# Attention with random features, a dense block and an eight-expert layer on one core: the first token search is spread anew over the products beside it

## The chip, the cores and the metric

One core of one Trainium2 chip runs the whole program in one launch. The metric is device time in microseconds (us), from the first to the last instruction of an execution and what lies around it. Five engines work at once, each through its own instructions in order: TensorE (PE in rows of the profile; PEld is its loading of weights), VectorE (DVE), ScalarE (ACT), GpSimd (POOL), and SyncE (SP), which here only issues DMAs. An engine waits for another through semaphores.

## The reference, cut to what matters

```python
# 1. attention with random features (4 batches, 8 heads, 576 positions, 64 wide, 128 features)
q_p, k_p = phi(q * scale), phi(k * scale)        # phi: exp of projections on omega, less their maximum
kv = einsum('bhsm,bhsd->bhmd', k_p, v);  z = sum(k_p, axis=2)
x = einsum(q_p, kv) / (einsum(q_p, z) + 1e-6)    # -> 2304 tokens of 512
# 2. dense block, 512 -> 2048 -> 512
h = x @ w_in;  x = (h * clip(h + 3, 0, 6) / 6) @ w_out
# 3. eight experts, each takes cap = 2304 // 8 = 288 tokens, by descending logit
logits = x @ w_gate
for idx in argsort(-logits.flatten()):           # best pair of token and expert first
    tok, e = idx // 8, idx % 8
    if assigned[tok] >= 0 or counts[e] >= cap: continue
    assigned[tok] = e; counts[e] += 1
for e in range(8):
    mask = assigned == e
    out[mask] = maximum(x[mask] @ w1[e], 0) @ w2[e]     # 512 -> 1024 -> 512
```

## The kernel before

Every large product is made three times, on a high and a low part of each operand (`mm3`, L208 to L210): high by high, low by high, high by low. A high part is a rounding copy on ScalarE, a low part a subtraction on VectorE or GpSimd. So each weight tile costs a "split" ahead of its products.

**Dense block.** Tokens go in four blocks of 512 and a short block of 256 (block 4, tiles 16 and 17). `steps` lists 16 jobs per block; `step(i)` makes the first product of job i (`st_A`), and some jobs later the second (`st_B`). The short block keeps its activations (`kept`: gHk, gLk) and makes its second products at the very end, in `rest()`: 16 jobs f, for each two token tiles j, for each three products of 128x512 (L694 and L696 in the two kernels): 96 products, each one `yield`. The weights of job f are split by `st_wo(f)` (L509 the high part oH on ScalarE, L510 the low part oL): on VectorE for f < OD and on GpSimd from there. oH and oL have three buffers, so the high part of job f + 3 waits until the products of job f are done. The finished tiles leave by `st_x` (L570 copy, L572 writes to `xd` in DRAM).

**Logits.** For the first LT = 14 token tiles they are dot products on VectorE (`st_dot`, L581), for the last four products on TensorE (`st_lg`, L611 and L612), which at the end are copied (L615), turned by four small transposes (L618) and added into `lg` (128 partitions x 18 tiles x 8 experts). L714 adds 0.0 to all of `lg`, so that no logit is a negative zero: the search compares the bits of the logits.

**Searches.** `finds()` is one generator for all eight searches. Each finds the expert that fills up next, the value that its 288th token has, and the list of its tokens:
- `begin()`: best logit of each token (L728 maximum), a sortable key, six digits of it, and `cmp`, the first digit compared with all its values (L755).
- `closest()`: six rounds, one per digit. In a round TensorE counts tokens per value with 18 small products (L771), VectorE compares the counts with 288 (`ge`, L773), TensorE sums that up (L776, the threshold product), VectorE takes the largest (dk, L780), makes the next digit's value (v, L783) and the next `cmp` (L755).
- `slots()` (L857, L858: the membership products) and `numbers()` (one-hot rows OH, L889; 18 products, L893) make the list of tokens `idx` (L898).

At each place where TensorE is about to get work of a search the generator yields a name: "cmp0", "cmp5" or "cmp6" ahead of the 18 counting products (by the width of the digit), "ge" ahead of the threshold product, "mem" ahead of membership, "OH" ahead of the 18 products of the list (in searches 0, 1, 6 and 7).

**What sets the order.** On TensorE these parts stand as the program writes them (`manual_schedule`); on the other engines a scheduler sorts by priority. Two tables tell how many products of other work stand behind each name. GAP0 holds for the first search, which is laced into `rest()`: `begin` products ahead of its first step, then after each named step as many as the table says. GAP holds for the searches 1 to 7, which are laced into the experts; there the count is in triples of products (`visit()`; an expert is 64 triples). Between them stands the only part without products of other work: after the first list, `fetch_x(0, ...)` gathers the first expert's rows from `xd` (three gathers, L917, issued by GpSimd), L923 copies the expert's number onto a gathered value so that the remaining weight loads come after the gathers (L925 reads it on SyncE, L928 and L909 load), N1 steps of the second search run, and `prep()` transposes the gathered rows (L943) and splits them (L944, L945). Then `mlp()` runs expert after expert, each with `prep` of the next at triples 56 to 62, and `finish` of the last. Weights We of an expert are split at L959 and L962 (w1), L963 and L966 (w2).

Of the kernel before, what the change touches and what calls it, by code (L numbers as in the profile page):

```python
# [9 lines left out]
ALU = mybir.AluOpType  # L10
# [10 lines left out]
def fused(tc, q, k, v, omega, w_in, w_out, w_gate, w1, w2, out):  # L21
    nc = tc.nc
# [8 lines left out]
    GI, NT = 20, 18  # L31
# [2 lines left out]

    ET = mybir.EngineType
    MN, IC = 16, 32
    OD, WG, ND, NE, XS = 4, 18, 3, 3, 3
    LB, LL, GB = 2, 3, 3

    LT = 14  # L40

    GAP0 = dict(begin=22, cmp5=8, cmp6=9, ge=3, mem=6, OH=0)


    W1C, W2C, Z0 = 4, 4, 2
    FZ, FS, PZ, PS = 6, 2, 56, 2
    HPF, RP, N1, GAP = 400, 30, 8, dict(cmp0=12, cmp5=4, cmp6=5, ge=1, mem=8, OH=9)
    DM = H * D
    DFF = w_in.shape[1]
    N = B * S  # L50
# [3 lines left out]
    with ctx:  # L54
# [9 lines left out]
        def ps(tag):  # L64
            if tag == "big":
                turn[0] += 1
                tag = ("s8", "kv", "kv")[turn[0] % 3]
            tag = TG.get(tag, tag)
            return pp.tile([P, 512], F32, tag=tag, name=tag, bufs=PA[tag])
# [457 lines left out]
        lg = cp.tile([P, NT, 8], F32, name="lg")  # L527
# [72 lines left out]
        def st_lg(i):  # L600

            ib, f = steps[i]
            gH, gL = gs[i]
            if "lg" not in keep:
                keep["lg"] = ps("tp")
            nl = (NT - LT) * P

            o = keep["lg"][:16, 0:nl - 2 * P] if ib < NB else keep["lg"][:16, nl - 2 * P:nl]
            w = wgp[:, f].rearrange("p a e -> p (a e)")
            c = slice((LT - 4 * ib) * P if ib < NB else 0, len(blocks[ib]) * P)  # L610
            nc.tensor.matmul(o, w, gH[:, c], start=f == 0, stop=False, skip_group_check=True)  # L611
            nc.tensor.matmul(o, w, gL[:, c], start=False, stop=f == NF - 1, skip_group_check=True)  # L612
            if ib == NB and f == NF - 1:
                t8 = mp.tile([16, nl], F32, name="lgT", bufs=1)
                nc.vector.tensor_copy(t8, keep["lg"][:16, :nl])  # L615
                pt = ps("tp")
                for j in range(NT - LT):
                    nc.tensor.transpose(pt[:, 16 * j:16 * j + 16], t8[:, j * P:(j + 1) * P], ident[:16, :16])  # L618
                p4 = pt[:, 0:16 * (NT - LT)].rearrange("p (t a e) -> p t a e", t=NT - LT, a=2)
                nc.vector.tensor_copy(lg[:, LT:NT], p4[:, :, 0])  # L620
                nc.vector.tensor_tensor(lg[:, LT:NT], lg[:, LT:NT], p4[:, :, 1], ALU.add)

        def st_B(i):
            ib, f = steps[i]
# [21 lines left out]
        def step(i):  # L646
# [23 lines left out]
            if LB <= i < NB * NF + LB:  # L670
                if i - LB >= (NB - 1) * NF and LT < 4 * NB:
                    st_lg(i - LB)
                st_B(i - LB)
            if i < len(steps) and ib == 1:
                st_wgp(f, wT)
            if i >= NB * NF + LL:
                st_lg(i - LL)
# [32 lines left out]
        mp_.close()  # L710
        rp = ctx.enter_context(tc.tile_pool(name="rp", bufs=2))
        wt, cs, opn, eidx = CT["wt"], CT["cs"], CT["opn"], CT["eidx"]

        nc.vector.tensor_scalar(lg, lg, 0.0, None, ALU.add)  # L714

        bc_e = lambda a: a.unsqueeze(2).to_broadcast([P, NT, E])
        small = lambda name, shape, dt=F32, bufs=2: rp.tile(list(shape), dt, tag=name, name=name, bufs=bufs)
# [305 lines left out]
        route = finds()  # L1023
        wait, placed = [GAP0["begin"]], False
        with tc.manual_schedule(engines={ET.PE}):
            for _ in more:
                wait[0] -= 1
                if wait[0] < 0 and not placed:
                    with tc.high_priority(offset=400):
                        z = next(route)  # L1030
                    placed, wait[0] = z == "first", GAP0.get(z, 0)
                    if z == "mem":
# [78 lines left out]
```

## Time and profile before

| | |
|---|---|
| median of three runs | 982.41 us (979.4 to 983.05) |
| profiled execution | 982.19 us, its span 980.1 us |
| busy, of the span | TensorE 907.6 us (93%), VectorE 640.7 (65%), ScalarE 495.9 (51%), GpSimd 481.4 (49%) |
| last product of `rest()` ahead of the first search | 623.64 us |
| first list of tokens | 659.30 us |
| first product of the first expert | 675.74 us |

The profile shows one execution. Its busy times are sums over stages with different limits, so a stretch is read from the timelines: each row is an instruction, or several equal ones, with its start, its length, and in brackets how long its engine was idle ahead of it and what ended that. The granted clock of TensorE is 1.00 at 2.4 GHz and 0.50 at 1.2 GHz.

### The profile page before, as it was taken

What the parts mean: (1) busy time and instruction counts of PE and PEld (TensorE: products, weight loads), DVE (VectorE), ACT (ScalarE), POOL (GpSimd) and SP (SyncE); (2) the same over time, 40 slices, a digit from 0 to 9 for tenths busy, and PEclk for the clock granted to TensorE, in tenths of its full rate; (3) what the DMA queues carried; (4) which work ended last, traced back from release to release, by engine and by line L of the source; (5) the groups of instructions that cost most, each with busy time, mean ns of one, the idle gap of its engine ahead of it and who ended that gap; (6) DMA issues with size and microseconds to landing.
All of it is one profiled execution on the core that took longest, in us unless ns stands there. A gap on an engine that the chain in (4) does not pass through costs nothing. (4 is left out here: it accounts for less than half of the span.)

```text
span 980.1 us, 16984 instructions
## 1 busy us (share of the span) xinstructions
PE 907.6 (93%) x6135; PEld 793.3 (81%) x6135; DVE 640.7 (65%) x1654; ACT 495.9 (51%) x1091; POOL 481.4 (49%) x447
## 2 busy tenths in 40 slices
PE   7998899989899999999999999876998999999996
PEld 6997788867678888878878889655997888888996
DVE  4779889778875662694369238555775758857442
ACT  5767788865454544534543457322352433534552
POOL 6579665346653533535444546342442434336542
PEclk9999899999999999999999999885997989989998
DMA  8855422012400000000010001024533516427600
GB/s 211 228 159 154 136 87 85 3 65 86 151 1 33 11 1 1 33 12 0 1 44 1 1 1 43 1 65 154 196 110 112 197 34 213 133 90 252 189 25 25
DMA packets 74852, 81.93 MB, mean 84 GB/s; under 512 B 27016, under 2 KB 59784, under 8 KB 74640
## 3 DMA queue, kind: packets, MB, share of 16 engines
q1 hardware_dynamic: 71536, 71.15, 23.0%
q0 software_dynamic: 3072, 9.44, 3.2%
q8 instruction: 48, 0.79, 0.3%
q10 hardware_dynamic: 160, 0.26, 0.1%
q14 instruction: 36, 0.29, 0.1%
HBM read 71.39 MB, written 9.45 MB: 82 GB/s over the span
## 5 line engine op out<-in xcount | busy, mean ns | idle before, releaser
L502 POOL TENSOR_TENSOR iL<-W,iH 128x512 fp32r<-128x512 f32 x80 | 112.7, 1410 | 96.0 <-ACT iH L501 86.3
L962 POOL TENSOR_TENSOR iL<-We,iH 128x512 fp32r<-128x512 f32 x63 | 84.9, 1349 | 143.9 <-ACT iH L959 137.2
L510 POOL TENSOR_TENSOR oL<-W,oH 128x512 fp32r<-128x512 f32 x60 | 81.8, 1363 | 112.7 <-ACT oH L509 112.4
L208 PE MATMUL kv<-xH,iH 128*128 128x512 f32 (+2 forms) x376 | 133.5, 355 | 2.1 <-ACT xH L520 1.8
L210 PE MATMUL kv<-xH,iL 128*128 128x512 f32 (+2 forms) x376 | 130.0, 346 | 2.5 <-POOL iL L502 2.5
L209 PE MATMUL kv<-xL,iH 128*128 128x512 f32 (+2 forms) x376 | 130.1, 346 | 0.9 <-DVE xL L521 0.9
L208 PE MATMUL pj<-oH,gH 128*128 128x512 f32 x256 | 102.4, 400 | 3.5 <-DVE xs L570 3.5
L210 PE MATMUL pj<-oH,gL 128*128 128x512 f32 x256 | 101.1, 395 | 0.0
L209 PE MATMUL pj<-oL,gH 128*128 128x512 f32 x256 | 100.8, 394 | 0.0
L501 ACT CAST iH<-W 128x512 fp32r<-128x512 f32 x80 | 49.7, 621 | 81.4 <-PE kv L209 50.0
L581 DVE SCALAR_TENSOR_TENSOR junk<-xs,wgb 128x512 f32<-128x512 f32 x96 | 88.8, 956 | 2.3 <-PE tp L596 2.2
L273 ACT ACTIVATE kp<-pj,bias 128x128 f32<-128x128 f32 x288 | 79.3, 410 | 18.0 <-DVE bias L265 14.5
L208 PE MATMUL pj<-hH,oH 128*128 128x288 f32 x256 | 85.2, 333 | 0.0
L959 ACT CAST iH<-We 128x512 fp32r<-128x512 f32 x64 | 39.5, 619 | 87.8 <-PE kv L209 43.4
L208 PEld LDWEIGHTS kv<-xH,iH 128*128 128x128 f32 x376 | 72.8, 194 | 12.5 <-issue 4.2
L210 PEld LDWEIGHTS kv<-xH,iL 128*128 128x128 f32 x376 | 72.9, 194 | 11.4 <-POOL iL L502 4.3
L209 PEld LDWEIGHTS kv<-xL,iH 128*128 128x128 f32 x376 | 73.0, 194 | 8.5 <-DVE xL L521 1.2
L209 PE MATMUL pj<-hL,oH 128*128 128x288 f32 x256 | 78.5, 307 | 1.0 <-DVE hL L984 1.0
L210 PE MATMUL pj<-hH,oL 128*128 128x288 f32 x256 | 78.1, 305 | 0.0
L544 DVE SCALAR_TENSOR_TENSOR kv<-r,kv 128x512 f32<-128x512 f32 (+1 forms) x54 | 34.7, 643 | 65.3 <-ACT r L543 65.1
L182 POOL TENSOR_TENSOR stg<-cg,stg 128x512 f32<-128x512 f32 x32 | 41.7, 1304 | 71.6 <-issue 30.4
L509 ACT CAST oH<-W 128x512 fp32r<-128x512 f32 x80 | 49.5, 620 | 45.5 <-PE pj L210 24.4
(400 smaller groups left out, 2399.1 us busy)
## 6 DMA issues: line engine op xcount, KB each, us to landing
We<-in_moe_w_dram SPq DMA_DIRECT2D x64, 512.0 KB, 7.3
stg<-in_moe_w_in_dram SPq DMA_DIRECT2D x16, 512.0 KB, 4.2
stg<-in_moe_w_out_dram SPq DMA_DIRECT2D x16, 512.0 KB, 3.5
ld<-in_k_dram SPq DMA_DIRECT2D x8, 512.0 KB, 4.9
vf<-in_v_dram SPq DMA_DIRECT2D x32, 128.0 KB, 3.8
ld<-in_q_dram SPq DMA_DIRECT2D x8, 512.0 KB, 5.1
xd<-xs SPq DMA_DIRECT2D x16, 256.0 KB, 2.2
wgb<-wgd SPq DMA_DIRECT2D x1, 2048.0 KB, 8.2
```

What stands on the lines that cost most here:

```text
L182: nc.gpsimd.tensor_tensor(lf, g.bitcast(F32), lf, ALU.mult)
L208: nc.tensor.matmul(o, aH, bH, start=first, stop=False, skip_group_check=True)
L209: nc.tensor.matmul(o, aH, bL, start=False, stop=False, skip_group_check=True)
L210: nc.tensor.matmul(o, aL, bH, start=False, stop=last, skip_group_check=True)
L273: nc.scalar.activation(kp[:, i, j], pjs[s // 4][:, s % 4], AF.Exp, bias=bias[:, i, j:j + 1])
L501: nc.scalar.copy(iH, wi)
L502: on_pool.append(nc.gpsimd.tensor_tensor(iL, wi, iH.bitcast(F32), ALU.subtract).ins)
L509: nc.scalar.copy(oH, wo)
L510: (nc.gpsimd if (ib > 0 if ib < NB else f >= OD) else nc.vector).tensor_tensor(oL, wo, oH.bitcast(F32), ALU.subtract)
L581: nc.vector.scalar_tensor_tensor(junk, x, 1.0, wgb[:, e], ALU.mult, ALU.mult, accum_out=d)
L959: nc.scalar.copy(iH, wi)
L962: (nc.vector if first and f == 0 else nc.gpsimd).tensor_tensor(iL, wi, iH.bitcast(F32), ALU.subtract)
```

## The change

Numbers in the tables, one constant of the splits, and the place of one addition change.

- **GAP0**: 32 products instead of 22 ahead of the first search; 6 instead of 8 behind each threshold product of a 5-bit round, 7 instead of 9 of a 6-bit round; 2 instead of 3 between counting and threshold; 9 instead of 6 ahead of membership; 12 instead of 0 ahead of the list. (A number n in the table makes n + 1 products. There are 96 in all, and none is left when the last entry comes.)
- **OD** 16 instead of 4: all splits of the short block are VectorE's.
- **The added zero**: the first 14 tiles of `lg` get it by an instruction of their own in `st_lg`, the other four within the addition that stands there. L714 is gone.
- **N1** 6 instead of 8: the transposes of the gathered rows come after three rounds of the second search instead of four.
- **GAP**: 6 instead of 8 ahead of membership, 7 instead of 9 ahead of the list, in the searches 1 to 7.

```diff
--- before.py
+++ after.py
@@ -34,17 +34,17 @@
 
     ET = mybir.EngineType
     MN, IC = 16, 32
-    OD, WG, ND, NE, XS = 4, 18, 3, 3, 3
+    OD, WG, ND, NE, XS = 16, 18, 3, 3, 3
     LB, LL, GB = 2, 3, 3
 
     LT = 14
 
-    GAP0 = dict(begin=22, cmp5=8, cmp6=9, ge=3, mem=6, OH=0)
+    GAP0 = dict(begin=32, cmp5=6, cmp6=7, ge=2, mem=9, OH=12)
 
 
     W1C, W2C, Z0 = 4, 4, 2
     FZ, FS, PZ, PS = 6, 2, 56, 2
-    HPF, RP, N1, GAP = 400, 30, 8, dict(cmp0=12, cmp5=4, cmp6=5, ge=1, mem=8, OH=9)
+    HPF, RP, N1, GAP = 400, 30, 6, dict(cmp0=12, cmp5=4, cmp6=5, ge=1, mem=6, OH=7)
     DM = H * D
     DFF = w_in.shape[1]
     N = B * S
@@ -617,8 +617,10 @@
                 for j in range(NT - LT):
                     nc.tensor.transpose(pt[:, 16 * j:16 * j + 16], t8[:, j * P:(j + 1) * P], ident[:16, :16])
                 p4 = pt[:, 0:16 * (NT - LT)].rearrange("p (t a e) -> p t a e", t=NT - LT, a=2)
+
                 nc.vector.tensor_copy(lg[:, LT:NT], p4[:, :, 0])
-                nc.vector.tensor_tensor(lg[:, LT:NT], lg[:, LT:NT], p4[:, :, 1], ALU.add)
+                nc.vector.tensor_scalar(lg[:, 0:LT], lg[:, 0:LT], 0.0, None, ALU.add)
+                nc.vector.scalar_tensor_tensor(lg[:, LT:NT], p4[:, :, 1], 0.0, lg[:, LT:NT], ALU.add, ALU.add)
 
         def st_B(i):
             ib, f = steps[i]
@@ -710,8 +712,6 @@
         mp_.close()
         rp = ctx.enter_context(tc.tile_pool(name="rp", bufs=2))
         wt, cs, opn, eidx = CT["wt"], CT["cs"], CT["opn"], CT["eidx"]
-
-        nc.vector.tensor_scalar(lg, lg, 0.0, None, ALU.add)
 
         bc_e = lambda a: a.unsqueeze(2).to_broadcast([P, NT, E])
         small = lambda name, shape, dt=F32, bufs=2: rp.tile(list(shape), dt, tag=name, name=name, bufs=bufs)
```

What the tables and the scheduler make of it, at three places. First VectorE between the last split activation of the short block (gLk) and the second step of `begin`. Before:

```order
L546 TENSOR_TENSOR gLk<-s_6448,gHk 128x256
L615 COPY lgT<-tp 16x512
L875 MEMSET aa 128x18
L620 COPY lg<-tp 128x32
L621 TENSOR_TENSOR lg<-lg,tp 128x32
L714 TENSOR_SCALAR lg<-lg 128x144
L728 TENSOR_REDUCE mx__6540<-lg 128x18
```

Now:

```order
L546 TENSOR_TENSOR gLk<-s_6448,gHk 128x256
L510 TENSOR_TENSOR oL<-W,oH 128x512
L615 COPY lgT<-tp 16x512
L510 TENSOR_TENSOR oL<-W,oH 128x512
L875 MEMSET aa 128x18
L621 COPY lg<-tp 128x32
L623 SCALAR_TENSOR_TENSOR lg<-tp,lg 128x32
L728 TENSOR_REDUCE mx__6558<-lg 128x18
L510 TENSOR_TENSOR oL<-W,oH 128x512
L730 TENSOR_TENSOR w__6560<-lg,mx__6558 128x144
```

Three splits (oL) have come in, ahead of the copy of the logits, behind it, and behind the maximum; the addition over all of `lg` is gone. Nine more splits stand further on, between the steps of the rounds, and four ahead of these rows as before.

Second TensorE, from the last of 18 counting products of the second round to its threshold product (tp is the small accumulator, pj the two accumulators of the short block). Before:

```order
L771 MATMUL tp_6604<-oh_6555,cmp_6602 32x8
L694 MATMUL pj_6499<-oL_6590,gHk_6034 128x512
L694 MATMUL pj_6499<-oH_6589,gLk_6184 128x512
L694 MATMUL pj_6500<-oH_6589,gHk_6034 128x512
L694 MATMUL pj_6500<-oL_6590,gHk_6034 128x512
L776 LDWEIGHTS onesu_4509
L776 MATMUL tp_6642<-ge_6640,onesu_4509 128x8
```

Now:

```order
L771 MATMUL tp_6621<-oh_6573,cmp_6619 32x8
L696 MATMUL pj_6499<-oH_6551,gLk_6184 128x512
L696 MATMUL pj_6500<-oH_6551,gHk_6034 128x512
L696 MATMUL pj_6500<-oL_6552,gHk_6034 128x512
L776 LDWEIGHTS onesu_4509
L776 MATMUL tp_6653<-ge_6651,onesu_4509 128x8
```

One product less stands between the two; behind the threshold product 7 follow instead of 9 (in the last two of these gaps 8 instead of 10). Between the row transposes L618 and the first counting product stand 13 products instead of 5, and between the last threshold product and membership 7 instead of 1.

Third, VectorE and SyncE ahead of the first expert. VectorE in the second search, before:

```order
L783 SCALAR_TENSOR_TENSOR v__7032<-v__6994,dk_7030,dg_7005 128x36
L923 SCALAR_TENSOR_TENSOR e2_6950<-xg_6948,ei_6865 1x1
L755 TENSOR_TENSOR cmp_7034<-v__7032,ta_4497 128x576
L773 TENSOR_SCALAR ge_7055<-tp_7036 32x8
L780 TENSOR_REDUCE dk_7059<-tp_7057 128x1
```

Now:

```order
L783 SCALAR_TENSOR_TENSOR v__7061<-v__7032,dk_7059,dg_7005 128x36
L755 TENSOR_TENSOR cmp_7063<-v__7061,ta_4497 128x576
L773 TENSOR_SCALAR ge_7084<-tp_7065 32x8
L923 SCALAR_TENSOR_TENSOR e2_6950<-xg_6948,ei_6855 1x1
L780 TENSOR_REDUCE dk_7088<-tp_7086 128x1
L783 SCALAR_TENSOR_TENSOR v__7090<-v__7061,dk_7088,dg_7005 128x36
```

The copy of the expert's number, e2, which waits for the last gather (xg), stood in the first round behind v; it now stands in the third, behind ge. SyncE before (xs is a finished tile of the short block, on its way to DRAM; We are the first expert's weights):

```order
L572 DMA xd<-xs 128x512 x16
L572 DMA xd<-xs 64x512 x2
L906 TENSOR_LOAD ei
L906 ISA x2
L909 ISA
L909 DMA We<-in_moe_w_dram 128x4x256
L909 ISA
L909 DMA We<-in_moe_w_dram 128x4x256
```

Now:

```order
L572 DMA xd<-xs 128x512 x16
L906 TENSOR_LOAD ei
L906 ISA x2
L909 ISA
L909 DMA We<-in_moe_w_dram 128x4x256
L909 ISA
L909 DMA We<-in_moe_w_dram 128x4x256
L572 DMA xd<-xs 64x512 x2
```

The two writes of 64 tokens stood ahead of the first two weight loads and now stand behind them. In the expert stage, the third expert's list stands 6 triples ahead of the first transposes of its rows instead of 8, the second expert's 23 instead of 27; the list of the fourth keeps its distance of 11.

## Rows read from the trace of the kernel before

**Rows 1.** Busy us, share of the span and instructions of each engine, from the page
```profile
PE 907.6 (93%) x6135; PEld 793.3 (81%) x6135; DVE 640.7 (65%) x1654; ACT 495.9 (51%) x1091; POOL 481.4 (49%) x447
```

**Rows 2.** Timeline of TensorE: start us, length us, operation, count, idle before and releaser
```profile
623.41 0.39 PE L694 MATMUL pj<-oL,gHk 128*128 128x512 f32 x1
623.64 0.40 PE L694 MATMUL pj<-oH,gLk 128*128 128x512 f32 x1
628.03 0.62 PE L771 MATMUL tp<-oh,cmp 128*32 128x8 bf16 x18 [3.99 <-issue]
...
633.88 0.61 PE L771 MATMUL tp<-oh,cmp 128*32 128x8 bf16 x18
```

**Rows 3.** Timeline of VectorE around the first search and in the second
```profile
606.95 0.68 DVE L510 TENSOR_TENSOR oL<-W,oH 128x512 fp32r<-128x512 f32 x1
...
622.81 0.19 DVE L620 COPY lg<-tp 128x32 f32<-128x32 f32 x1 [0.69 <-PE tp L618]
...
623.26 1.26 DVE L714 TENSOR_SCALAR lg<-lg 128x144 f32<-128x144 f32 x1
...
626.17 1.24 DVE L742 CAST v__6553<-di 128x36 bf16<-128x36 int32 x1
...
662.12 0.18 DVE L742 CAST v__6994<-di 128x36 bf16<-128x36 int32 x1
```

**Rows 4.** Timeline of GpSimd in the same stretches
```profile
626.01 1.36 POOL L510 TENSOR_TENSOR oL<-W,oH 128x512 fp32r<-128x512 f32 x1
...
664.45 1.27 POOL L962 TENSOR_TENSOR iL<-We,iH 128x512 fp32r<-128x512 f32 x1
```

**Rows 5.** Windows: stretch, its us, busy PE, PEld, DVE, ACT, POOL, granted clock, DMA
```profile
626.00:627.00 1.00, 0.00 (x0) 0.00 (x0) 1.00 (x3) 0.00 (x0) 1.00 (x2) 0.50 0.00 0
...
906.00:907.00 1.00, 1.00 (x6) 1.00 (x5) 0.00 (x0) 0.19 (x1) 0.70 (x2) 0.50 0.75 249
...
920.00:930.00 10.00, 10.00 (x78) 9.99 (x77) 3.44 (x9) 5.36 (x11) 6.35 (x6) 1.00 0.21 62
```

**Rows 6.** Timeline of TensorE, two counting steps that follow each other in full clock
```profile
637.94 0.61 PE L771 MATMUL tp<-oh,cmp 128*32 128x8 bf16 x18
...
642.01 0.61 PE L771 MATMUL tp<-oh,cmp 128*32 128x8 bf16 x18
```

**Rows 7.** Timeline of VectorE, the step v of two rounds without products between
```profile
668.69 0.26 DVE L783 SCALAR_TENSOR_TENSOR v__7061<-v__7032,dk,dg 128x36 bf16<-128x36 bf16 x1
...
670.79 0.26 DVE L783 SCALAR_TENSOR_TENSOR v__7090<-v__7061,dk,dg 128x36 bf16<-128x36 bf16 x1
```

**Rows 8.** Timeline of all engines, end of the first search
```profile
652.49 0.18 PE L776 MATMUL tp<-ge,onesu 64*128 64x8 bf16 x1
...
653.13 0.69 DVE L570 COPY xs<-pj 128x512 f32<-128x512 f32 x1
...
659.30 0.16 DVE L898 SCALAR_TENSOR_TENSOR idx<-tp,lo 96x3 int32<-96x3 f32 x1
```

**Rows 9.** Timeline of all engines, second search ahead of the first expert
```profile
664.18 1.61 DVE L783 SCALAR_TENSOR_TENSOR v__7032<-v__6994,dk,dg 128x36 bf16<-128x36 bf16 x1
...
666.84 0.15 DVE L923 SCALAR_TENSOR_TENSOR e<-xg,ei 1x1 int32<-1x1 int32 x1 [1.05 <-DMA xg<-xd,idx]
...
673.01 1.19 PE L943 MATMUL kv<-ident,xg 96*128 96x96 f32 x6 [0.37 <-DMA We<-in_moe_w_dram]
```

**Rows 10.** Timeline of ScalarE, a high part of the short block
```profile
624.07 0.62 ACT L509 CAST oH<-W 128x512 fp32r<-128x512 f32 x1 [1.32 <-PE pj L694]
```

**Rows 11.** Timeline of TensorE in the expert stage, four of its waits
```profile
694.61 1.08 PE L893 MATMUL tp<-mv,OH 128*96 128x6 bf16 x18 [0.76 <-DVE OH L889]
...
751.23 0.30 PE L943 MATMUL kv<-ident,xg 96*128 96x96 f32 x1 [0.78 <-DMA xg<-xd,idx]
...
821.20 0.16 PE L776 MATMUL tp<-ge,onesu 32*128 32x8 bf16 x1 [1.27 <-DVE ge L773]
...
903.68 1.08 PE L893 MATMUL tp<-mv,OH 128*96 128x6 bf16 x18 [1.43 <-DVE OH L889]
```

## The prediction, made before the changed kernel had run

> **What bounds the kernel now.** The page first: TensorE is busy for 93% of the span [rows 1], so most stages can gain only what its gaps and its slow clock hold. The change acts on one of them, so the rest is read from timelines between 620 us and 676 us, where the first expert's tokens are searched. Five stretches stand out there.
>
> First, a wait. The last product of the short block that stands ahead of the search starts at 623.64; then TensorE has nothing for 3.99 us until the search's first counting product at 628.03 [rows 2]. Meanwhile VectorE runs the chain that makes its operand: it takes the logits at 622.81, adds zero to all of them (1.26 us), and later casts the first digits in 1.24 us [rows 3]. The same cast takes 0.18 us in the second search [rows 3]. Beside the slow one GpSimd runs a 1.36 us split of the short block [rows 4].
>
> Second, the clock. In that wait it falls to 0.50 (the 1.2 GHz level), and one round of the search, from its first counting product to the next, takes 5.85 us (628.03 to 633.88); a later one at full clock takes 4.07 [rows 2, 5, 6].
>
> Third, the rounds. One holds 13 products of the short block at 0.23 us (two starts in [rows 2]): 4 between counting and threshold, 9 (in two rounds 10) behind the threshold. Without products between, a round takes 2.10 us, from one step v to the next [rows 7]. So TensorE's own queue, not VectorE, paces the rounds: about 2 us of each are cover that the chain doesn't need.
>
> Fourth, from the last threshold product (652.49) to the index list (659.30 + 0.16 = 659.46) [rows 8] it is VectorE's chain, 6.97 us, with one 0.69 us copy of a finished block in it. TensorE is out of products there.
>
> Fifth, the second search's first four rounds stand on TensorE ahead of the transposes of the gathered rows. The step v of its first round starts at 664.18 and takes 1.61 us, and behind it VectorE waits for the gather, until 666.84. The transposes begin at 673.01, 13.55 us after the index list and 6 after the gather [rows 9].
>
> **The change part by part.** Sums go against the profiled execution, 982.2 us (span 980.1 and 2.1 around it); the median of the runs is 982.4.
>
> *Products moved.* Of the 71 products between the first counting and the last threshold product 55 stay (gaps of 3, and 7 or 8). Ten move ahead of the search, into the 3.99 us, and six behind it, where TensorE had no work. 16 x 0.233 = 3.7 us. This holds if a round still hides the chain: 4.07 - 3 x 0.233 = 3.37 us against 2.10, plus one split on VectorE, 0.6 us ([rows 3]: 0.68 with its tail), or two, 1.2. Bound: 0 if splits eat all the cover; **-3.7** taken, as 3.3 still fits.
>
> *Start of the chain.* Gone: the 1.26 us zero add (14 of its 18 columns of tokens go ahead of it, among the short block's splits, where the products on TensorE cover them, 1.26 us at most if they don't; the other four get it within an addition that was there) and the excess of the cast, 1.24 - 0.18, since GpSimd has no splits left. That is -2.3. Added: three splits stand between the last logits and the counting. The first delays the copy of the logits by 0.3, the second the addition by 0.3 more, the third sits between the maximum and the comparison. It needs a high part from ScalarE that waits for a buffer held by an earlier product; before, that cast ran at 624.07 [rows 10]. So about 0.4 of waiting and 0.6 of its own. Sum -2.3 + 1.6 = **-0.7**; bounds -1.7 (nothing waits) and +0.5 (it waits a buffer's turn longer). TensorE then lacks work for some 1.2 us instead of 3.99.
>
> *Clock.* A wait of 1.27 us in the expert stage left the clock at full; one of 1.43 us was followed by 0.50 some 3 us later [rows 5, 11]. At 1.2 I take it to stay, and the first round's excess, 5.85 - 4.07, goes: **-1.8**; bound 0. The Trainium skill (TensorE: Matmul & The Clock Gate, What's actually happening) says that the gate is free-running, so the same gap may cost one run the clock and spare it in another; by that this term may be 0 in some executions.
>
> *Tail.* The 0.69 copy leaves the chain ahead of the membership but stands behind it, ahead of the scan; the six products cover most of either. -0.1. The 18 products of the index list may find the clock at full; half of the 0.7 us that would save. Together **-0.4** (bounds +0.3, -0.8). On SyncE the write of tokens 64x512 x2 moves behind the first two weight loads; the gather waits for it. It would start the gather up to 1 us late. The gather is not last, though: it lands 6 us ahead of the transposes [rows 9], of which the next part takes 3.2. So 0; bound +1.
>
> *Two jobs.* Transposes stand one round sooner: -2.1 [rows 7]. The wait for the gather moves from the first round to behind the third threshold, by when the gather has landed: without it the next step would have followed v's end, 665.79, and it followed 666.84 instead, -1.1. v's own excess, 1.61 against 0.26 in other rounds [rows 7], lies beside GpSimd's split of 664.45 [rows 4], which follows the gathers as before: kept; bound -1.35 more. The Trainium skill (SBUF — State Buffer, Who interferes with whom) has the first to issue hold the shared port; v started 0.27 us ahead of that split and was slow all the same, so the trace doesn't bear that out here. By the rule v would be free whenever it stays first, and the sum 974.3. Together **-3.2**.
>
> *Paid later.* The round taken out is run within expert 0, on a busy TensorE: 0.61 + 0.18 and a slowed neighbour [rows 6, 8], **+0.9**. Being behind, it moves the third expert's index list from 8 product triples ahead of its transposes to 6; the order shows this. That expert waits for its gather already (0.78 us for the last piece at 751.23 [rows 11]), so two triples at 0.385 us (26 in 10 us [rows 5]) come out as idle time: **+0.8**. The gap ahead of the index products falls from 10 triples to 8 in three searches. Two of them wait for VectorE now, 0.76 and 1.43 us [rows 11], and wait 0.77 longer: **+1.5** (bounds 0 and +2.3). The gap ahead of the membership product falls by two in all later searches; in the trace TensorE waits for that product in the first search only, so 0, bound +0.8 for a search whose operand comes late.
>
> Sum: -3.7 - 0.7 - 1.8 - 0.4 - 3.2 + 0.9 + 0.8 + 1.5 = -6.6: 982.2 - 6.6 = **975.6 us**.
>
> **The rivals.** *The clock falls anyway*, in the 1.2 us wait, or in the index wait of the second search, which grows from 0.76 to 1.5, past the 1.43 that cost it. For: both lie at the edge of what the rows show. Against: 1.27 spared it. Each costs the first round's 1.8: 977.4 for one, **979** for both.
>
> *The splits bind the rounds*, the case on the other side. VectorE works in order: a split between two chain steps holds the chain until ScalarE's cast, and that waits for a product which stands behind the same chain. It decides once a split waits over 0.7 us (3.37 - 2.10 - 0.6). TensorE then idles in every round, the clock stays at half, and a round takes 5.85 - 3 x 0.43 = 4.6 us. Five rounds at +0.5, none of the 3.7 and 1.8: 982.2 - 0.7 + 2.5 - 0.4 - 3.2 + 3.2 = **984**, up to 990 if the third split waits a round too. For: twelve splits stand in the chain's queue. Against: the buffers are three deep, and each needed product stands a gap earlier.
>
> *v runs free*: if the moved write starts the gathers later, GpSimd's split falls behind v, which then takes 0.26: **974.3**. The shared port's rule of the Trainium skill, above, says so even without that. For: 0.27 us decide it. Against: the row itself.
>
> *Given back later*: nothing in the expert stage starts sooner by itself. If two more gathers or index lists come late, each waits some 1.4 us and pays the half clock, 1.8, behind it: 975.6 + 2 x 3.2 = **982**. For: those waits stand in the trace today, and the change tightens two kinds of them. Against: only one gather comes closer to its use.
>
> **How the numbers follow.** Forecast 0.48, v free 0.08, clock 0.26, given back 0.10, bound rounds 0.08. A measurement of this kernel can tell about 0.5%, 4.9 us. Faster by that (under 977.5): the forecast's case, v free and a little of the clock's, 0.58. Within: most of the clock's, given back, and half of the bound rounds, 0.36. Slower (over 987.3): 0.06. Range: down to 971 (v's block, the start and the tail at their good ends: -1.35 - 1.0 - 0.4, and 2 less in the two gaps), up to 982, which leaves out the bound rounds and the worse half of given back.
>
> **What would show it.** Right: the wait ahead of the first counting product near 1.2 us; clock 1.00 in the first round; rounds of about 3.4 us; last threshold near 646; index list near 653; transposes near 663 and the first expert's products 10 us sooner than at 675.74. Then the expert stage 3 us longer than before, with the growth in the gather of the third expert and the index products. Wrong: rounds still near 4 us with VectorE named ahead of the counting (the splits), 0.50 in the first round (the clock), transposes waiting for the gather (the moved write), or a stage of experts that is longer by far more than 3 us, or shorter, since its waits fall anew.

## The result, and the profile after

The changed kernel takes 968.22 us (median of four runs, 964.04 to 971.14) against 982.41, a ratio of 0.9858 (95% interval 0.9811 to 0.9906); measured again beside other kernels (e5 below) 0.9853 (0.9836 to 0.9869). Faster was right, but the gain is 14 us where 6.6 were forecast, and the time lies below the range. The profiled execution is the slowest of the four, 971.14 us with a span of 969.4. Kernels below are compared by their ratio to the kernel before, measured on the same chip, since before itself moves between 979.9 and 983.6 us from chip to chip.

The page first (busy us, share and instructions of each engine), against [rows 1]: TensorE is still busy for 93%.

```profile
PE 901.8 (93%) x6135; PEld 787.7 (81%) x6135; DVE 641.6 (66%) x1666; ACT 496.2 (51%) x1091; POOL 466.8 (48%) x435
```

Timeline of TensorE after, from the end of the short block to the first expert (start us, length us, operation, count, idle before and releaser); these answer to [rows 2, 6, 8, 9]:

```profile
628.92 0.40 PE L696 MATMUL pj<-oH,gHk 128*128 128x512 f32 x1
630.34 0.59 PE L771 MATMUL tp<-oh,cmp 128*32 128x8 bf16 x18 [1.02 <-issue]
...
633.68 0.61 PE L771 MATMUL tp<-oh,cmp 128*32 128x8 bf16 x18
...
637.02 0.61 PE L771 MATMUL tp<-oh,cmp 128*32 128x8 bf16 x18
...
649.20 0.18 PE L776 MATMUL tp<-ge,onesu 64*128 64x8 bf16 x1
...
665.65 0.55 PE L943 MATMUL kv<-ident,xg 96*128 96x96 f32 x2 [0.37 <-issue]
668.16 0.90 PE L943 MATMUL kv<-ident,xg 96*128 96x96 f32 x4 [1.96 <-DMA xg<-xd,idx]
...
670.05 0.61 PE L208 MATMUL kv<-xH,iH 128*128 128x288 f32 x1
```

The wait ahead of the first counting product is 1.02 us instead of 3.99. A round takes 3.34 us (630.34 to 633.68 to 637.02) instead of 5.85 and 4.07. New is a wait of 1.96 us for the gathered rows in the middle of the transposes. VectorE in the same stretch, against [rows 3, 7, 8, 9]:

```profile
629.54 0.17 DVE L742 CAST v__6571<-di 128x36 bf16<-128x36 int32 x1
...
655.37 0.16 DVE L898 SCALAR_TENSOR_TENSOR idx<-tp,lo 96x3 int32<-96x3 f32 x1
...
660.83 0.26 DVE L783 SCALAR_TENSOR_TENSOR v__7032<-v__6994,dk,dg 128x36 bf16<-128x36 bf16 x1
```

The slow cast is gone (0.17 instead of 1.24), the list stands at 655.53, and the step v of the second search takes 0.26 us instead of 1.61.

Where the time went, in the two profiled executions and in a second one of the changed kernel (e5). The ten products moved ahead of the search (2.33 us) are counted with the search:

| stretch | forecast | after | second profile |
|---|---|---|---|
| up to the last product ahead of the search (623.64, 628.92, 627.61), less 2.33 | 0 | +2.95 | +1.64 |
| from there to the list (659.46, 655.53, 655.62), with the 2.33 | -6.6 | -6.9 | -5.5 |
| list to the first expert's first product (675.74, 670.05, 669.25) | -3.2 | -1.8 | -2.65 |
| from there to the end of the span | +3.2 | **-5.0** | **-4.2** |

The first line is mostly scatter: the fourteen kernels of this case that run the same program up to there have -0.3 to +3.8 in it, and e2, which is the kernel before up to there, +0.75; that the change itself costs up to 1 us there is not excluded. The first search came out as forecast. The last line is the miss: where I had put 3.2 us of loss in the expert stage, 4 to 5 were gained. That is not one lucky profile: the six kernels with these N1 and GAP and GpSimd's splits (after, and e2, e5, e8, e9 and e10 below) have stages of 294.7 to 301.5 us in their profiles, the two with the old ones (before, e1) 304.4 and 302.7.

One row for the first 278 us of that stage, from the first expert's first product (us, busy PE, PEld, DVE, ACT, POOL, granted clock, DMA). Before:

```profile
675.74:953.74 278.00, 263.12 (x2329) 247.22 (x2330) 181.86 (x616) 116.74 (x241) 120.68 (x101) 0.94 0.42 140
```

After:

```profile
670.05:948.05 278.00, 263.32 (x2388) 247.41 (x2387) 184.16 (x626) 120.55 (x248) 123.55 (x103) 0.97 0.44 148
```

And in the second profile of the changed kernel (e5):

```profile
669.25:947.25 278.00, 265.12 (x2382) 249.36 (x2381) 182.26 (x625) 119.80 (x247) 122.72 (x102) 0.95 0.44 148
```

TensorE is busy for the same 263 us in the first two but gets through 59 instructions more: the granted clock is 0.97 on the mean instead of 0.94. In windows of 2 us, the time at 0.50 adds up to 35 us before, 19 after and 27 in the second profile. At 0.50 a busy TensorE does half the work, so by this estimate the clock gave back (35 - 19) / 2 = 8 and (35 - 27) / 2 = 4 us, of the size of the gain in the stage. And the longest waits are others: nine of over 0.7 us before, 11.7 us in all, eight after (9.4) and seven in the second profile (7.5). The groups of waits in the stage show it (waiting and awaited line, us in total, times, longest). Before:

```profile
PE tp L776 <- DVE ge L773: 6.0, 4, 2.0
PE kv L943 <- DMA xg<-xd,idx: 3.8, 4, 1.6
PE tp L893 <- DVE OH L889: 2.4, 3, 1.4
```

After:

```profile
PE tp L776 <- DVE ge L773: 4.8, 7, 1.9
PE kv L943 <- DMA xg<-xd,idx: 3.9, 4, 1.4
PE pj L209 <- DVE hL L984: 3.2, 4, 1.3
...
PE tp L893 <- DVE OH L889: 0.5, 1, 0.5
```

The two waits for OH of [rows 11], 0.76 and 1.43 us, which the prediction let grow, became 0.48 and nothing.

### The profile page after: what moved, and what is told of

It reads as the page before. It is cut to its first block, busy times and chain, and to the rows that moved or that the text cites. A ratio compares the mean times of both kernels' runs of the same rounds, so it can differ in the third digit from the quotient of the medians.

```text
span 969.4 us, 16981 instructions
## 1 busy us (share of the span) xinstructions
PE 901.8 (93%) x6135; PEld 787.7 (81%) x6135; DVE 641.6 (66%) x1666; ACT 496.2 (51%) x1091; POOL 466.8 (48%) x435
## 5 line engine op out<-in xcount | busy, mean ns | idle before, releaser
L510 POOL TENSOR_TENSOR oL<-W,oH 128x512 fp32r<-128x512 f32 x48 | 66.2, 1380 | 95.8 <-ACT oH L509 95.6
```

The lines of the kernel that those rows point to most:

```text
L510: (nc.gpsimd if (ib > 0 if ib < NB else f >= OD) else nc.vector).tensor_tensor(oL, wo, oH.bitcast(F32), ALU.subtract)
```

## Experiments: which edit, and which mixture

Two theories at first. A: the edits add, and the 5 us of the expert stage belong to N1 and GAP (the numbers of the change that set the second search against the first expert, and the searches against the experts). B: they come from when the stage starts, or from luck with the clock.

**e1, the first search alone.**

```diff
-    HPF, RP, N1, GAP = 400, 30, 6, dict(cmp0=12, cmp5=4, cmp6=5, ge=1, mem=6, OH=7)
+    HPF, RP, N1, GAP = 400, 30, 8, dict(cmp0=12, cmp5=4, cmp6=5, ge=1, mem=8, OH=9)
```

> The edits of the first search alone (GAP0, OD, the zero add); N1 and GAP as before. Between the profiled executions of before and after, the stretch from the short block to the first index list gained 6.8 us, the stretch from the list to the first expert's first product 1.8, and the expert stage behind it 5.0. Theory A (the parts add, and the 5.0 belong to the shorter gaps and the sooner transposes): this kernel has only the first gain, 982.4 - 6.8 = 975.6, with an expert stage near 304 us. Theory B (the 5.0 come from when the stage starts, or from luck with the clock, whatever the table): near 970.6, with a stage near 299.

Measured 0.9941 (0.9920 to 0.9961): 5.8 us gained, with an expert stage of 302.7 us. That is A.

**e2, N1 and GAP alone**: the kernel before with the line of after.

> Only N1 = 6 and the shorter GAP, on the kernel before. Theory A: 1.8 from the sooner transposes and 5.0 in the expert stage, 975.6, stage near 299 us. Theory B: 1.8 alone, 980.6, stage near 304 us. The prediction's own step had this part at 3.2 gained ahead of the experts and 3.2 paid in them: 982.

Measured 0.9919 (0.9893 to 0.9946): 7.9 us gained, with a stage of 294.7 us. The product of both ratios is 0.9860, the kernel after 0.9853. A holds, and this part alone had been forecast at nothing.

**e3 and e4, N1 and GAP apart**, each on the kernel after: e3 with N1 = 8, e4 with mem = 8 and OH = 9.

> The kernel after with N1 = 8: the fourth round of the second search stands ahead of the transposes again. If that round is worth what the traces show between list and first product, 1.8 us, less the round's own 0.9 within the experts: 968.2 + 0.9 to 1.8 = 969 to 970. If the position of the third expert's list (8 instead of 6 triples ahead of its transposes) is worth more than that, it is as fast as after or faster, 967 to 968, with less waiting for gathers (2.5 us at the third expert after).

> The kernel after with the old GAP (8 triples ahead of membership, 10 products' worth ahead of the list, as before), N1 = 6. Theory A with the gaps as the cause of the 5.0: 968.2 + 5.0 = 973, stage near 304 us, and more time at half clock (before 34 us of the stage, after 20). The prediction's step (shorter gaps make the index products wait 1.5 longer): 966.7. Theory B: 968.

e3 0.9886 (0.9863 to 0.9908), e4 **1.0109** (1.0088 to 1.0130): with the sooner transposes but the old gaps the whole change would have cost 11 us. No theory had forecast that. The timeline of TensorE in e4 at the third and fourth expert shows it:

```profile
744.63 0.42 PE L943 MATMUL kv<-ident,xg 96*128 96x96 f32 x1 [4.44 <-DMA xg<-xd,idx]
...
788.97 0.30 PE L943 MATMUL kv<-ident,xg 96*128 96x96 f32 x1 [2.50 <-DMA xg<-xd,idx]
```

and the groups of its waits in the stage:

```profile
PE kv L943 <- DMA xg<-xd,idx: 15.9, 13, 4.4
```

How many triples of products stand between an expert's list and the first transposes of its rows, counted in the order of the program:

| | N1, GAP | 3rd expert | 4th | 5th | 6th | ratio |
|---|---|---|---|---|---|---|
| e1 (and before) | 8, old | 8 | 11 | 14 | 17 | 0.9941 |
| e3 | 8, new | 14 | 19 | 24 | 29 | 0.9886 |
| after | 6, new | 6 | 11 | 16 | 21 | 0.9853 |
| e4 | 6, old | 0 | 3 | 6 | 9 | 1.0109 |

N1 moves every later list behind by 8 triples; the shorter gaps bring the second expert's list forward by 4 and each one after it by 2 more. So the two edits are one: a search is nearly as long as an expert (59 to 61 of 64 triples in these four, from the third expert's list on), and a list that comes late makes the later ones late. The wait for gathers in the stage grows from nothing (e3) over 1.4 to 3.9 (e1 has 2.7, the two profiles of after 3.9 and 1.4) to 15.9 us (e4). The prediction counted the order for the kernel after, saw 6 instead of 8, and was right by that one number; it never asked what the gaps were worth against the rounds.

## Experiments: why the stage gained

**e5 to e8.** e5 is the kernel after again. e6 takes the gaps two triples further down, e7 has the old gaps and a shorter search, e8 puts the write of the last tokens back ahead of the first weights.

```diff
-    HPF, RP, N1, GAP = 400, 30, 6, dict(cmp0=12, cmp5=4, cmp6=5, ge=1, mem=6, OH=7)
# e6:
+    HPF, RP, N1, GAP = 400, 30, 6, dict(cmp0=12, cmp5=4, cmp6=5, ge=1, mem=4, OH=5)
# e7:
+    HPF, RP, N1, GAP = 400, 30, 6, dict(cmp0=12, cmp5=3, cmp6=5, ge=1, mem=8, OH=9)
```

For e8 (the two lines go in both places where they stand):

```diff
-                    if z == "mem":
-                        fetch_w(0, rs[0], 0, Z0)
...
+        fetch_w(0, rs[0], 0, Z0)
         fetch_x(0, rs[0])
```

> The kernel after, unchanged, beside the three others of this call. If the two halves of the change multiply (ratios 0.9941 for the first search alone and 0.9919 for N1 and GAP alone), the ratio to before is 0.986: 966.3 where before is 980.0.

> After with the gaps of GAP shorter by another two triples each (mem 4, OH 5; N1 stays 6). The list of the third expert then stands 12 triples ahead of the transposes of its rows instead of 6, that of the fourth 19 instead of 11. Theory D (the distance between a list and its transposes decides): the waits for gathers in the expert stage go from 3.9 us to under 0.5, time at half clock falls with them, and the total by 4 to 6: 961 to 963. Rival (each gap is there to hide a chain on VectorE, as the prediction had it): the membership and list products wait 0.77 longer in each search, four lists and seven memberships: plus 3 to 6, which cancels it: 966 to 969.

> After with the old gaps for membership and list (mem 8, OH 9), but one triple less behind each threshold product of a 5-bit round (cmp5 3 instead of 4), so that a search is as long as in after within a triple. The list of the third expert stands 4 triples ahead of its transposes (after 6, the kernel with the old gaps 0), the fourth 10 (11, 3). Theory D: within 2 of after, 967 to 970, gather waits 4 to 6 us. Rival (the gaps at membership and list themselves did it, by the place where GpSimd's splits meet the search's steps on VectorE): near the kernel with the old gaps, 990.

> After with the first weight loads of the first expert issued behind the write of the last tokens, as they stood before. Theory (the write landed 5.3 us after issue behind 1 MB of weights instead of 2.3, and held the gathers): gathers are issued about 4 us sooner, the wait of 1.96 us ahead of the transposes goes, first product of the first expert about 2 us sooner, 966. Rival (weights then come late): their splits hold the first products and the gain is under 0.5.

e6 0.9912 (0.9885 to 0.9939), e7 0.9887 (0.9862 to 0.9913), e8 0.9844 (0.9829 to 0.9860). In e7 a search is about as long as in after, and e4's loss is gone with 3 us between e7 and after: most of it was the length of a search, wherever it is saved. But distance is not all. In e6 no wait for gathers is left, and it is 6 us slower than after. Its longest waits are one of 4.16 us for hL (the low part of an expert's activation), one of 2.94 for a GpSimd split, which stands behind the issues of three gathers on its own engine, and one for a membership product. The last in the timeline (VectorE, GpSimd and TensorE):

```profile
790.64 1.02 POOL L1010 DMA_INDIRECT out_dram<-y,idx  x1 [0.71 <-ACT y L1008]
...
791.33 1.67 DVE L813 SCALAR_TENSOR_TENSOR mem<-vf,sel 128x18 bf16<-128x18 f32 x1
...
791.68 1.27 POOL L962 TENSOR_TENSOR iL<-We,iH 128x512 fp32r<-128x512 f32 x1
...
793.13 0.18 PE L857 MATMUL tp<-mem,ta 128*128 128x36 bf16 x1 [2.22 <-DVE mem L814]
```

The step mem, 0.16 us in most searches, took 1.67 and ended when the GpSimd split beside it did (793.00 and 792.95). TensorE waited for it, for 2.22 us. The wait for hL stands behind two steps of the next search that meet splits in the same way (L739 at 830.50 and 832.97, 1.29 and 1.94 us instead of 0.15):

```profile
836.12 0.61 PE L209 MATMUL pj<-hL,oH 128*128 128x288 f32 x1 [4.16 <-DVE hL L984]
```

Theory D (distance) falls as the only cause.

In e8 the write of the last tokens was meant to let the gathers start sooner, and did. The issues of the gathers (count, ns min, median and max, first and last start) in after:

```profile
L917 POOL DMA_INDIRECT xg<-xd,idx x3: 917/923/1106, 660.7 to 663.3; - x3
```

In e8, where the list is ready 0.5 us sooner:

```profile
L917 POOL DMA_INDIRECT xg<-xd,idx x3: 920/1105/1127, 656.0 to 658.9; - x3
```

The first product of the first expert stands 12.5 us behind the list instead of 13.6 to 14.5. The total is not to be told from after: in its profile the stage is 301.5 us long instead of 299.4 and 300.2.

**What the waits have in common.** The waits of e6 led to theory C: they come from VectorE steps that meet a GpSimd split. Before, around the two lists of [rows 11] (timeline of VectorE and GpSimd):

```profile
692.13 1.33 POOL L962 TENSOR_TENSOR iL<-We,iH 128x512 fp32r<-128x512 f32 x1 [2.05 <-ACT iH L959]
692.23 1.31 DVE L879 TENSOR_TENSOR jj<-aa 128x54 f32<-128x54 f32 x1
...
899.48 1.93 DVE L879 TENSOR_TENSOR jj<-aa 128x54 f32<-128x54 f32 x1
900.02 1.30 POOL L962 TENSOR_TENSOR iL<-We,iH 128x512 fp32r<-128x512 f32 x1
```

The same two steps in after, where no split meets them:

```profile
690.11 0.21 DVE L879 TENSOR_TENSOR jj<-aa 128x54 f32<-128x54 f32 x1
...
888.00 0.20 DVE L879 TENSOR_TENSOR jj<-aa 128x54 f32<-128x54 f32 x1
```

So the wait for OH of 0.76 and 1.43 us was not a gap too short, as the prediction took it, but a step ahead of OH held by 1.1 and 1.7 us (in the second case a split of VectorE's own behind it, too: 1.50 us at 901.43 instead of 0.42, beside the next GpSimd split). Such meetings are not luck of a run either. e1, which shares its tables with before, has the waits of before at the same steps, within 0.02 us (timeline of TensorE in e1):

```profile
731.08 0.16 PE L776 MATMUL tp<-ge,onesu 32*128 32x8 bf16 x1 [1.91 <-DVE ge L773]
...
813.85 0.16 PE L776 MATMUL tp<-ge,onesu 32*128 32x8 bf16 x1 [1.27 <-DVE ge L773]
...
851.82 0.16 PE L776 MATMUL tp<-ge,onesu 32*128 32x8 bf16 x1 [2.05 <-DVE ge L773]
...
896.41 1.09 PE L893 MATMUL tp<-mv,OH 128*96 128x6 bf16 x18 [1.45 <-DVE OH L889]
```

against 1.91, 1.27 and 2.05 and 1.43 before (the first and third at 737.64 and 859.15, the others in [rows 11]). VectorE steps of the stage that are over 0.3 us longer than the shortest of their kind exceed it by some 25 us in all, in before (26 steps) as in after (25); every one of them overlaps a GpSimd split. The change didn't make fewer of them; it moved the excess onto other steps. Where it falls counts and not its sum: in e6 it is only 16 us.

**e9 to e12.** e9 and e10 undo two edits of the first search on the kernel after (OD = 4; GAP0 as before). e11 and e12 test theory C.

```diff
-                    (nc.vector if first and f == 0 else nc.gpsimd).tensor_tensor(iL, wi, iH.bitcast(F32), ALU.subtract)
# e11:
+                    (nc.vector if True else nc.gpsimd).tensor_tensor(iL, wi, iH.bitcast(F32), ALU.subtract)
# e12:
+                    for z in range(2):
+                        z = slice(z * 2, z * 2 + 2)
+                        (nc.vector if first and f == 0 else nc.gpsimd).tensor_tensor(iL[:, z], wi[:, z], iH[:, z].bitcast(F32), ALU.subtract)
```

> After with OD = 4: twelve splits of the short block go back to GpSimd. Theory (a GpSimd split beside a VectorE step costs that step about 1.1 us, as in the cast of 1.24 against 0.18; twelve of them meet six rounds that have about 1.2 us of cover each): the start of the chain loses 1.0, some rounds up to 1 each: 969.9 to 973 where after is 968.9. Rival of the prediction (the splits on VectorE bind the rounds): OD = 4 is faster, 966 to 968.

> After with the old GAP0; the other edits stay. The prediction's terms: 16 products of 0.233 back in the rounds, 3.7, and the wait ahead of the first counting product back at about 3 us, which costs the clock in the first round, 1.8, where after had it at full in one of two profiles: 968.9 + 3.7 + 0.9 to 1.8 = 973.5 to 974.4. Rival (the spread over the jobs is worth nothing and the 7 us of the first search come from the start of the chain): under 970.

> After with all splits of the experts' first weights (L962) on VectorE, none on GpSimd. Theory (in the trace of after, 24 VectorE steps of the expert stage are 0.4 to 2.6 us longer than the shortest of their kind, 25 us in all, each beside a GpSimd split; they make TensorE's waits for ge, hL, mem and OH, 9 us): the excess goes, those waits fall under 4 us, time at half clock falls, 961 to 965. Rival (VectorE gets 63 x 0.6 = 38 us more work and loses 25, and a split of 0.6 in front of a search step holds it as well): waits as now or longer, 969 to 975.

> After with each GpSimd split of L962 as two instructions of half the columns. Theory (a VectorE step that meets one is held to its end): excess per step at most about 0.7 us instead of 1.3, the waits for ge, hL, mem and OH fall from 9 to about 5 us, 964 to 967. Rival (a held step waits for both halves, or meets twice as many): as after, 968 to 970.

e9 0.9857 (0.9820 to 0.9893): no difference to after, so neither theory; which engine makes these twelve splits can't be told from the time. e10 0.9940 (0.9919 to 0.9960): the spread of the products is worth 8 us where its terms, with the clock's, were 5.5 (in the profiles, counted as in the table of stretches, the one up to the list is 6.7 and 5.3 us longer in e10 than in after and e5). e12 0.9845 (0.9829 to 0.9861): no difference; its two halves follow each other without a pause, the waits for ge, hL, mem and OH are 8.1 us (after 9.1), and the excess of the long steps is still 22, with up to 1.7 in one step: a step is not held by half as much, as the rival had it. Of the cause it tells no more.

e11 **0.9806** (0.9776 to 0.9836): faster than after by half a per cent, though VectorE is busy for 651.3 us instead of 641.6. No VectorE step in the stage is longer than the shortest of its kind by 0.3 us any more. The waits for hL and OH are gone; those for gathers are 3.5 us (3.9 and 1.4 in the two profiles of after), so the gain is not that GpSimd is free to issue gathers. Its waits in the stage:

```profile
PE kv L943 <- DMA xg<-xd,idx: 3.5, 3, 1.3
PE tp L776 <- DVE ge L773: 2.2, 3, 0.9
...
PE tp L857 <- DVE mem L814: 0.8, 1, 0.8
PE tp L771 <- DVE cmp L755: 0.4, 1, 0.4
```

**e13 to e16**, all without GpSimd's splits in the stage: e13 with N1 = 8, e14 with the write first (as e8), e15 with both, e16 with the old N1 and GAP (as e1).

> e11 (no GpSimd splits in the expert stage) with N1 = 8: the third expert's list stands 14 triples ahead of its transposes instead of 6, so the 3.5 us of waits for gathers in the stage go; a round more ahead of the transposes, 2.1, of which 0.9 come back from the stage. Theory D (distance): ratio to before 0.978, 960. If the gathers' waits are worth no more than the round: as e11, 0.9806.

> e11 with the write of the last tokens ahead of the first weights. The write lands in 2.3 us instead of 5.4, the gathers start up to 4 us sooner. With GpSimd's splits this was worth 0.1% (0.9844 against 0.9853); expected here the same, 0.9797 to 0.981, that is no difference that the run can tell.

> e11 with N1 = 8 and the write ahead of the weights. The gather lands by the time the fourth round is done; distances as in e13. If both terms are real: 0.977, 959.

> The first search's edits with the old N1 and GAP (as e1), and no GpSimd splits in the expert stage. Theory C (the tables' gain in the stage came from where the splits meet the search's steps): without splits the old tables are as good as the new ones but for gathers, ratio within 0.003 of e11, 0.981 to 0.984. Theory D (distance decides): the old tables stay 0.9 per cent behind the new ones, 0.989 to 0.990, with waits for gathers.

| N1, GAP | with GpSimd's splits | without |
|---|---|---|
| 8, old | e1 0.9941 | e16 0.9764 (0.9736 to 0.9792) |
| 8, new | e3 0.9886 | e13 **0.9738** (0.9712 to 0.9764) |
| 6, new | e5 0.9853 | e11 0.9806 (0.9776 to 0.9836) |

e14 0.9796 (0.9772 to 0.9820), e15 0.9743 (0.9722 to 0.9764): the write first is worth nothing that can be told here either.

The column without splits turns the order around: the tables of the change are the slowest of the three. e16 answers to both theories. D is wrong by 12 us; C had the new tables level with the old, and they are 4 us behind. What gained 8.6 us with the splits (e5 against e1) loses 4.1 without them (e11 against e16). The intervals of e11 and e16 overlap a little, so the 4.1 alone is hardly clear of noise; that the 8.6 don't come back is. Waits in the stage of e16:

```profile
PE kv L943 <- DMA xg<-xd,idx: 3.5, 4, 1.3
PE tp L893 <- DVE dk L780: 0.8, 3, 0.3
PE tp L893 <- DVE aa L875: 0.3, 1, 0.3
```

and its row of the first 278 us:

```profile
674.64:952.64 278.00, 268.73 (x2466) 254.71 (x2464) 197.05 (x693) 125.44 (x259) 43.08 (x45) 0.98 0.45 148
```

against that of e11:

```profile
668.17:946.17 278.00, 269.91 (x2444) 255.40 (x2443) 196.71 (x694) 122.42 (x253) 42.94 (x42) 0.96 0.44 147
```

The stage takes 281.7 us in e16 and 291.9 in e11; ahead of it e11 gains 4.6 (list to first product 13.8 against 18.3). No experiment separates what makes up the 10.3 us; in the rows, waits of TensorE are 3.4 more (ge, mem and cmp, which e16 doesn't have; those for gathers are 3.5 in both), the clock is 0.96 instead of 0.98, by estimate 2% of 278 or 5.6 us, and one round is run within the stage. e13 parts N1 from GAP. It differs from e11 in N1 alone, has no wait for gathers and none for ge in the stage, and is 6.7 us faster; against e16 it differs in GAP alone, 2.5 us, within their intervals. The best version is e13 at 955.7 us, with e15 beside it (955.2): both are faster than before by 2.6%, than after by over one.

## Why the prediction was wrong, step by step

*Products moved, -3.7*: right. Rounds of 3.34 were forecast as about 3.4 us, the last threshold, forecast near 646, stood at 649.20, which with the 2.95 of the stretch ahead of it is right, and e10 puts the edit at 8 us with the clock's part in it.

*Start of the chain*: right in its parts. The wait is 1.02 for 1.2, the cast 0.17. That the splits bind the rounds, the rival on the slow side, did not happen: rounds hide them, and e9 shows no difference for OD.

*Clock, -1.8, at 0.26 for its rival*: that was a coin. The granted clock around the first round in after (windows of 2 us, columns as above):

```profile
631.00:633.00 2.00, 2.00 (x9) 1.39 (x10) 1.22 (x6) 0.62 (x1) 0.00 (x0) 1.00 0.03 8
```

and in e1, with the same program up to there and a wait of 1.01 us:

```profile
629.00:631.00 2.00, 2.00 (x6) 1.56 (x5) 1.11 (x3) 0.14 (x1) 0.00 (x0) 0.50 0.00 0
```

Of the fourteen kernels that start the search alike, seven have a first round of 3.32 to 3.34 us and seven one of 4.2 to 4.6. The same wait can cost the clock or spare it, and the chance should have been one half. Where it costs it, the first two rounds take 8.0 us together instead of 6.7, so the price is 1.3 us and not 1.8. The Trainium skill (TensorE: Matmul & The Clock Gate, What's actually happening), cited in the prediction, has a free-running gate; these fourteen agree.

*Tail and the moved write, -0.4 with 0 for the write*: the write was mis-sized. DMA issues of the stretch, the last tokens' write (count, KB each, us to landing), before:

```profile
xd<-xs SPq DMA_DIRECT2D x2, 128.0 KB, 2.3
```

and after:

```profile
xd<-xs SPq DMA_DIRECT2D x2, 128.0 KB, 5.3
```

Behind 1 MB of weights it landed 5.3 us after its issue, the gathers were issued 5.1 us behind the list instead of 1.1, and the transposes waited 1.96 us for them. e8, with the write ahead again, issues them 1.0 us behind the list. The bound of +1 was the length of the queue's issue; the transfers in front of it were left out.

*Two jobs, -3.2*: -1.8 and -2.65. v ran in 0.26 us after all, as its rival had it and for the rival's reason: the moved write made the gathers late, and they moved GpSimd's split far behind v, which stands at 660.83 (GpSimd in after):

```profile
660.66 1.11 POOL L917 DMA_INDIRECT xg<-xd,idx  x1 [30.66 <-PE tp L776]
...
664.23 1.28 POOL L962 TENSOR_TENSOR iL<-We,iH 128x512 fp32r<-128x512 f32 x1
```

The gain was eaten by the wait of the transposes for them; e8, where they are not late, has -3.8 (12.5 us against 16.3).

*Paid later, +0.9 + 0.8 + 1.5 = +3.2*: the step that failed; the stage took 5.0 and 4.2 us less. The third expert's gather was to cost 0.8 us more: its waits were 2.21 us before, 2.49 after and 1.42 in the second profile. The index products had the wrong sign, 1.9 less instead of 1.5 more, because the row that priced them was read as a chain too long for its gap, and it was a step held by a GpSimd split. And the term left out the largest part. Which steps of a search are held was itself set by the tables; moving each search by some triples dealt that anew, and with fewer long waits went less time at half clock. That is the last clause under "What would show it" ("or shorter, since its waits fall anew"), which I named and gave no price or chance; the range's low end had no gain in the stage in it. That the gain depends on GpSimd's splits is shown by its turning into a loss when they are taken away from GpSimd. That it comes by the held steps rests on the rows (with the splits there, every long step overlaps one; without them, there is no long step), and how much of it each held step and the clock made is not shown.

With the splits away from GpSimd, the sign of the whole term is right: there N1 and GAP cost 4 us together (e11 against e16, hardly clear of noise). Its parts are not: the waits for gathers are the same in both, and there is none for OH. Distance does cost, as the prediction had it, but that shows against e13, where the third expert's list stands 14 triples ahead and not 6: 6.7 us for N1 alone. With GpSimd's splits the other effect, 13 us between the two columns (8.6 + 4.1), hid all that.

## What to carry to other kernels

A wait in a trace has a length and a cause, and only the cause says how an edit will move it: look at whether the step that ends it is as long as its like elsewhere before pricing it by the distance to it. If two engines slow each other where they meet, an edit of a table of positions is a new deal of meetings; take the meetings away first, then tune the table, since its best setting is another one then. And edits that shift the same chain against its deadline (here N1 and GAP) are priced together, since one alone may cost more than both gain.

## What the runs showed of the hardware

A VectorE step of 0.16 us can be held to the end of a GpSimd split beside it, even if the profile has it start first: 791.33 against 791.68 in e6, 899.48 against 900.02 before (jj, 1.93 us instead of 0.20, till 901.41, the split till 901.32). What the prediction overlooked at v, and what holds for all such steps of the stage (five in before, six in after): GpSimd was in the issue of a gather or scatter when the step began, and the split followed that issue within 0.03 us. For v in before (at 664.18, its split at 664.45):

```profile
663.51 0.92 POOL L917 DMA_INDIRECT xg<-xd,idx  x1 [0.31 <-issue]
```

An issue alone holds nothing: v in after began in one (660.66, above) that no split followed, and took 0.26 us; in e11 96 steps of the stage began in one of GpSimd's 45 issues, and none is over 0.15 us longer than the shortest of its kind. The Trainium skill (SBUF — State Buffer, Who interferes with whom) has the first to issue hold the shared port. By the start of the split these rows don't agree; by that of the issue ahead of it they might, and no run here shows what holds a step from the one into the other.

Sixty-three splits of 1.3 us on GpSimd cost more than sixty-three of 0.69 us on the busier VectorE (e5 0.9853, e11 0.9806).

Waits of one length were followed by half clock in one place and not in another, and in one execution and not in another: 1.91 us for ge at 737.64 before, and the granted clock was 0.50 from 738.7 on; 1.95 us for ge at 812.95 in after, and it stayed at 1.00; in e5, the same kernel, the same wait of 1.95 us at 811.39, and it was 0.50 from 812 to 815.
